# Attention into two expert layers: later routing constants, earlier weight splits, products with v behind six chunks, a turned chunk order

## The chip, the cores and the metric

The kernel runs on one core of a Trainium2 chip. The metric is the device time of one execution in microseconds; a kernel's time is the median of its runs. The five engines have in-order queues: TensorE (PE, with its weight loads PEld), VectorE (DVE), ScalarE (ACT), GpSimd (POOL), and SyncE (SP), which here only issues DMA.

## The reference

Three stages follow one another; the change touches the first and its hand-over to the second. The first is attention on 4 batches of 8 heads with 576 rows of 64 columns:

```python
def _attn_ref(q, k, v, tau):
    scale = 1.0 / np.sqrt(q.shape[-1])
    scores = scale * np.matmul(q, k.transpose(0, 1, 3, 2))
    thresh = np.max(scores, axis=-1, keepdims=True) - tau
    scores = np.where(scores >= thresh, scores, -1000000000.0)
    scores = scores - np.max(scores, axis=-1, keepdims=True)
    attn = np.exp(scores)
    attn = attn / (np.sum(attn, axis=-1, keepdims=True) + 1e-09)
    return np.matmul(attn, v).astype(np.float32)
```

The second sends each of the 2304 rows to the best of 8 experts (`np.maximum(xe @ w1[e], 0.0) @ w2[e]`, times the gate's probability), the third runs 4 further experts on every row and adds them up, weighted by `domain_probs`.

## The kernel before

Attention takes the heads two by two: 16 pairs, four to a batch. A pair's 576 rows of scores for two heads are cut into nine row chunks of 128: four for each head, and one (`None` in `full`, line 758) that holds the last 64 rows of both heads. `attention` (line 500) records all engines by hand in one loop over t = 0 to 148 (line 1100); one turn is called a step here, and t mod 9 its place in the pair. In step t, in this order:

- ACT takes the exponential of chunk t-1 (`expp`, line 794), PE multiplies q by k for chunk t+1 (`mm_s`, lines 776 and 777), DVE copies chunk t out of PSUM with its row maximum (`maxx`, line 785), and POOL makes the threshold `nm` from it (line 788).
- `late_setup` gives one piece (line 1125): small constants for routing, on POOL, then DVE.
- The next pair's q and k are split into high and low parts on POOL (`prep`, lines 569 and 572), and PE transposes those of the pair after this one in eight groups, `k0` to `l1` (line 698), two of them at place 1 and one at each place to 7. ACT copies each out (lines 646 to 696).
- DVE masks and sums chunk t-2 (`mask`, line 805).
- PE transposes the masked chunk t-4 (`transp`, lines 824 to 842), and ACT copies it into `PT` (lines 828 to 843).
- `xq` gives a step of a finished batch's routing (gate products, transposes, scatter into `xs`).
- At places 0 and 5 PE runs one half of an earlier pair's products of `PT` with v (`pv_items`, lines 859 and 865): 18 matmuls on 288 of the pair's 576 columns. DVE copies the result in the next step (line 876). `push_pv` (line 1088) queues both halves at place 4, after all nine chunks; the second half of a batch's fourth pair starts `after_batch`, that is routing.

All PE transposes and products of this loop go through one pool of four PSUM buffers in turn (`ps()`, line 516); the scores have two buffers of their own.

At the end of the loop the first weights of the first expert layer are split into high and low parts on POOL (`dosplit` and `split`, lines 360 and 362, at steps 140 and 143); the PE then works through the last chunks, the last pair's products, the last routing (`first_group`, line 1068) and the first products with these weights.

Of the kernel before, what the change touches and what calls it, by code (L numbers as in the profile page):

```python
# [11 lines left out]
F32 = mybir.dt.float32  # L12
F32R = mybir.dt.float32r
# [19 lines left out]
def kernel(  # L33
# [14 lines left out]
    nc = tc.nc  # L48
# [43 lines left out]
    def late_setup():  # L92
        nc.gpsimd.affine_select(
            out=tri, in_=ones, pattern=[[1, 128]], compare_op=ALU.is_gt, fill=0.0, base=0, channel_multiplier=-1
        )
        nc.gpsimd.iota(i8, pattern=[[1, 8]], base=0, channel_multiplier=0, allow_small_or_imprecise_dtypes=True)
        yield
        nc.vector.tensor_scalar(w8, i8, -1.0, 8.0, op0=ALU.mult, op1=ALU.add)
# [108 lines left out]
    def rank_consts():  # L207
        nc.gpsimd.iota(i16, pattern=[[1, 16]], base=0, channel_multiplier=0, allow_small_or_imprecise_dtypes=True)
        for r in range(8):
            nc.gpsimd.memset(cap[:, r : r + 1], float(CAP[r]))  # L210
        yield
        nc.vector.scalar_tensor_tensor(ck, reg0, -8.0, w8, op0=ALU.mult, op1=ALU.add)
        nc.vector.tensor_scalar(th, bc(i8, 1, 8), float(XW), None, op0=ALU.mult)
        nc.vector.tensor_tensor(th, th, bc(cap, 2, 8), op=ALU.add)
        nc.vector.tensor_tensor(low, bc(i8, 2, 8), bc(i8, 1, 8), op=ALU.is_gt)
# [133 lines left out]
    def place(i):  # L349
        return i < 4 or i // 2 % 2 == 1  # L350

    def raw_tile(i):
        return pools["wa" if place(i) else "wb"].tile([128, 1024], F32, tag="raw", name="raw", bufs=2)

    def split(raw, eH, eL, i):
# [144 lines left out]
    def attention(actx):  # L500
# [11 lines left out]
        NWARM = (36, 3, 3, 3)  # L512
        ET0 = 140
        g = nc.gpsimd
# [119 lines left out]
        def qk_groups(p):  # L634
# [62 lines left out]

            return [k0, k1, k2, q0, q1, q2, l0, l1]

# [58 lines left out]
        full = [(1, 0), (0, 0), (1, 1), (0, 1), (1, 2), (0, 2), (1, 3), (0, 3)]  # L758

        def order(p):  # L760
            return [None] + full if p == NPR - 1 else full + [None]

# [268 lines left out]
        setup = late_setup()  # L1031
        filling = fill(xe, 5)
        qk, pv, xq, dq, fq, po = deque(), deque(), deque(), deque(), [], []
        last = NPR - 1
# [52 lines left out]

        def push_pv(p, halves, deadline):
            b = p // 4
            for n, hf in enumerate(halves):  # L1090
                mm, ev = pv_items(p, hf)
                for f in mm:
                    pv.append((f, None, deadline))
                fin = None
                if p % 4 == 3 and n == len(halves) - 1:
                    fin = (lambda: after_batch(b)) if p != last else first_group
                pv.append((ev, fin, deadline))

        t = 0
        while t < NTT + LT + LP:  # L1100
# [5 lines left out]
            if t < NTT:  # L1106
# [16 lines left out]
                fpop()  # L1123
                if 11 <= t < 36:
                    next(setup, None)
# [15 lines left out]
            if u >= 0:  # L1141
                pp, ss = divmod(u, 9)
                if pp != last and ss == 8:
                    push_pv(pp, (0, 1), 9 * (pp + 2) + LT - 1)
                if pp == last and ss == 4:
                    push_pv(pp, (0,), t + 2)
            for _ in range(-(-len(qk) // (8 - s)) if 0 < s < 8 else 0):
                qk.popleft()()
            if 0 <= t - LT < NTT:
                transp(t - LT)  # L1150
            if t == ET0:
                dosplit(0, "g", "g")
                fetch(2)
            if t in (ET0 + 1, ET0 + 2):
                x_tr(*early["xr"][t - ET0 - 1], early["x"], ps)
            if t == ET0 + 3:
                dosplit(1, "g", "g")
                fetch(3)
            for _ in range(min(len(xq), 1 if t < NTT + LM else 3)):
                if xq[0] in frees or not fq and not busy and (xq[0] is not early_start or t >= 9 * last):  # L1160
                    xq.popleft()()
            if pv and (t % 9 in (0, 5) or t > 9 * last):
                d = pv[0][2]
# [477 lines left out]
```

## Time and profile before

| | |
|---|---|
| median of three runs | 1321.33 us (1319.15 to 1322.68) |
| the profiled execution | 1320.02 us, span 1318.1 us |
| busy share of the span | PE 98%, PEld 88%, DVE 66%, POOL 64%, ACT 49% |
| mean granted clock of TensorE | 0.995 of full speed |
| chain that ended last | PE 53%, waits for nothing shown 2%, POOL 1% |

The loop of attention fills the span from about 10 to 321 us, the first expert layer follows to about 550 us, the second takes the rest. PE is busy in nine tenths or more of nearly every slice of the span, so that what PE loses anywhere is lost at the end. A busy PE is not a PE at its peak: ends of matmuls are modelled, and a short wait can hide behind them. A wait is read from the row in which an engine starts: the square bracket at its end holds the idle time before it and what ended that.

### The profile page before, as it was taken

The page shows a single profiled execution, that of the slowest core. Times are in us where ns is not written, and L with a number is a line of the kernel's source. Part 1 is how long each engine was busy: PE and PEld are TensorE (multiplying, and loading weights), DVE is VectorE, ACT ScalarE, POOL GpSimd, SP SyncE. Part 2 cuts the span into 40 slices and gives each one's busy share as a digit, 9 for nine tenths or more (in the row PEclk, how much of TensorE's full clock was granted, in tenths as well). Part 3 has the DMA queues.
Part 4 walks back from the last instruction along what each step waited for, and adds up shares of the span by engine and source line. Part 5 has one row for each costly group of instructions (what it writes and reads, how often), then busy time and mean ns, then how long its engine had stood idle before and what let it go on. Part 6 is the DMA issues. An engine that isn't in the chain of part 4 may idle for free.

```text
span 1318.1 us, 22000 instructions
## 1 busy us (share of the span) xinstructions
PE 1294.5 (98%) x7928; PEld 1155.9 (88%) x7928; DVE 863.5 (66%) x1773; ACT 640.6 (49%) x1239; POOL 848.2 (64%) x937
## 2 busy tenths in 40 slices
PE   8999999999999999999999999999999999999997
PEld 7788788786999999989999999999999999999996
DVE  8888889887834357765655557556565675555654
ACT  7788888875554455643333334433333343333321
POOL 8776877754485442677667755777676667766642
PEclk8999999999999999999999999999999999999999
DMA  4542112113674556631221111222211122221101
GB/s 147 181 145 77 60 57 77 33 34 109 194 216 154 165 175 186 201 102 67 88 70 64 65 64 65 80 86 103 68 65 64 64 73 80 90 93 66 64 16 48
DMA packets 131534, 127.15 MB, mean 96 GB/s; under 512 B 17920, under 2 KB 110080, under 8 KB 131424
## 3 DMA queue, kind: packets, MB, share of 16 engines
q1 hardware_dynamic: 127968, 116.22, 27.8%
q0 software_dynamic: 3456, 9.51, 1.9%
q8 instruction: 63, 1.03, 0.3%
q14 instruction: 47, 0.39, 0.1%
HBM read 107.28 MB, written 18.42 MB: 95 GB/s over the span
## 4 chain that ended last, share of the span: by engine, by line
PE 53%; issue 2%; POOL 1%; ACT 0%; POOLq 0%; DVE 0%; ACTq 0%; DVEq 0%
PE w L370 9%; PE w L368 9%; PE w L369 9%; PE w L1487 8%; PE w L1489 8%; PE w L1488 8%; POOL out_dram L194 0%; POOL v2hl L1251 0%; POOL hl L1251 0%; ACT v2hl L1290 0%; ACT hl L1266 0%; POOLq L1636 0%; ACT yc L1301 0%; POOL pad L193 0%; DVE w L1495 0%
## 5 line engine op out<-in xcount | busy, mean ns | idle before, releaser
L1251 POOL TENSOR_TENSOR v2hl<-raw,v2hl 128x1024 fp32r<-128x1024 f32 x48 | 116.0, 2417 | 183.3 <-ACT v2hl L1290 183.3
L1562 DVE SCALAR_TENSOR_TENSOR y<-w,big,y 128x512 f32<-128x512 f32 x252 | 184.7, 747 | 75.1 <-PE w L370 73.9
L1487 PE MATMUL w<-yc,hl 128*128 128x384 f32 x672 | 225.6, 336 | 3.2 <-DVE y L425 1.8
L1489 PE MATMUL w<-yc,hl 128*128 128x384 f32 x672 | 225.5, 336 | 0.0
L1488 PE MATMUL w<-yc,hl 128*128 128x384 f32 x672 | 225.3, 335 | 0.0
L370 PE MATMUL w<-v2hl,g 128*128 128x512 f32 x576 | 224.8, 390 | 0.0
L368 PE MATMUL w<-v2hl,g 128*128 128x512 f32 x576 | 224.7, 390 | 0.0
L369 PE MATMUL w<-v2hl,g 128*128 128x512 f32 x576 | 224.4, 390 | 0.0
L1500 ACT ACTIVATE g<-w 128x384 fp32r<-128x384 f32 x192 | 94.4, 492 | 231.1 <-DVE w L1495 158.5
L1290 ACT CAST v2hl<-raw 128x1024 fp32r<-128x1024 f32 x48 | 50.4, 1050 | 220.2 <-PE w L370 204.5
L362 POOL TENSOR_TENSOR hl<-raw,hl 128x1024 fp32r<-128x1024 f32 x40 | 96.6, 2417 | 93.2 <-ACT hl L358 82.4
L1501 DVE SCALAR_TENSOR_TENSOR g<-w,g 128x384 fp32r<-128x384 f32 x192 | 106.5, 555 | 58.8 <-ACT g L1500 54.1
L805 DVE SCALAR_TENSOR_TENSOR P<-sb,nm,E 128x576 f32<-128x576 f32 x144 | 131.6, 914 | 10.4 <-POOL nm L788 3.7
L1487 PEld LDWEIGHTS w<-yc,hl 128*128 128x128 f32 x672 | 126.2, 188 | 5.7 <-issue 1.9
L370 PEld LDWEIGHTS w<-v2hl,g 128*128 128x128 f32 x576 | 108.1, 188 | 23.1
L1488 PEld LDWEIGHTS w<-yc,hl 128*128 128x128 f32 x672 | 126.2, 188 | 1.7
L369 PEld LDWEIGHTS w<-v2hl,g 128*128 128x128 f32 x576 | 108.1, 188 | 21.4
L368 PEld LDWEIGHTS w<-v2hl,g 128*128 128x128 f32 x576 | 108.2, 188 | 21.1
L1489 PEld LDWEIGHTS w<-yc,hl 128*128 128x128 f32 x672 | 126.2, 188 | 0.0
L788 POOL TENSOR_SCALAR nm<-nm,sc 128x1 f32<-128x1 f32 x144 | 82.3, 571 | 67.5 <-DVE sb L785 43.1
L1251 POOL TENSOR_TENSOR hl<-sx,hl 128x1024 fp32r<-128x1024 f32 x47 | 113.3, 2411 | 14.1 <-ACT hl L1266 14.1
L1251 POOL TENSOR_TENSOR hl<-raw,hl 128x512 fp32r<-128x512 f32 x94 | 95.5, 1038 | 38.8 <-ACT hl L1266 38.5
(308 smaller groups left out, 3023.1 us busy)
## 6 DMA issues: line engine op xcount, KB each, us to landing
raw<-in_moe_w_dram SPq DMA_DIRECT2D x168, 512.0 KB
xs<-zrow SPq DMA_DIRECT2D x32, 256.0 KB
kt<-in_k_dram SPq DMA_DIRECT2D x16, 256.0 KB
qt<-in_q_dram SPq DMA_DIRECT2D x16, 256.0 KB
vt<-in_v_dram SPq DMA_DIRECT2D x16, 256.0 KB
xrow<-xs SPq DMA_DIRECT2D x15, 256.0 KB
kt<-in_k_dram SPq DMA_DIRECT2D x16, 32.0 KB
qt<-in_q_dram SPq DMA_DIRECT2D x16, 32.0 KB
```

The lines of the kernel that those rows point to most:

```text
L362: e.tensor_tensor(hl[:, 1, :], raw, hl[:, 0, :].bitcast(F32), op=ALU.subtract)
L368: nc.tensor.matmul(o, lhsT=aH, rhs=bH, start=first, stop=False)
L369: nc.tensor.matmul(o, lhsT=aH, rhs=bL, start=False, stop=False)
L370: nc.tensor.matmul(o, lhsT=aL, rhs=bH, start=False, stop=last)
L805: nc.vector.scalar_tensor_tensor(P, sb, nm[:, 1:2], e, op0=ALU.is_le, op1=ALU.mult, accum_out=a)
L1251: e.tensor_tensor(o, a, b_, op=ALU.subtract)
L1487: nc.tensor.matmul(o, lhsT=aH, rhs=bH, start=first, stop=False, skip_group_check=True)
L1488: nc.tensor.matmul(o, lhsT=aH, rhs=bL, start=False, stop=False, skip_group_check=True)
L1489: nc.tensor.matmul(o, lhsT=aL, rhs=bH, start=False, stop=last, skip_group_check=True)
L1500: nc.scalar.activation(o[0], src, AF.Relu)
L1501: return lambda: nc.vector.scalar_tensor_tensor(o[1], src, 0.0, o[0].bitcast(F32), op0=ALU.max, op1=ALU.subtract)
L1562: nc.vector.scalar_tensor_tensor(d, w3(o), s_, d, op0=ALU.mult, op1=ALU.add)
```

## The change

Five edits, all in or around the loop of attention:

1. `late_setup` starts at step 20, not 11, and waits a step more between the POOL and the DVE instructions of its two groups of constants.
2. The first two weight splits start at step 137 (`ET0`), not 140, and `split_early` gives two of their eight pieces in each step. The low part of each is computed in two halves of 512 columns.
3. A pair's first half of the products with v is queued once six of its row chunks are transposed, and runs at place 1; the second half runs at place 5. Routing of a finished batch so starts four steps sooner.
4. In odd batches, whose columns lie in another order, the chunks are taken in the order 1, 2, 3, 0 and the second half of the columns comes first.
5. For the last pair, `l1` and `l0` change places.

```diff
--- before.py
+++ after.py
@@ -95,6 +95,7 @@
         )
         nc.gpsimd.iota(i8, pattern=[[1, 8]], base=0, channel_multiplier=0, allow_small_or_imprecise_dtypes=True)
         yield
+        yield
         nc.vector.tensor_scalar(w8, i8, -1.0, 8.0, op0=ALU.mult, op1=ALU.add)
         nc.vector.tensor_scalar(reg0, i8, float(NTOK), None, op0=ALU.mult)
         nc.vector.tensor_copy(base, reg0)
@@ -209,6 +210,7 @@
         for r in range(8):
             nc.gpsimd.memset(cap[:, r : r + 1], float(CAP[r]))
         yield
+        yield
         nc.vector.scalar_tensor_tensor(ck, reg0, -8.0, w8, op0=ALU.mult, op1=ALU.add)
         nc.vector.tensor_scalar(th, bc(i8, 1, 8), float(XW), None, op0=ALU.mult)
         nc.vector.tensor_tensor(th, th, bc(cap, 2, 8), op=ALU.add)
@@ -352,6 +354,17 @@
     def raw_tile(i):
         return pools["wa" if place(i) else "wb"].tile([128, 1024], F32, tag="raw", name="raw", bufs=2)
 
+    def split_early(i):
+        raw = raws.pop(i)
+        hl = hls[i] = pools["wa"].tile([128, 2, 1024], F32R, tag="hl", name="hl", bufs=2)
+        nc.gpsimd.tensor_scalar(hl[:, 0, :], raw, 1.0, 1.0, op0=ALU.mult, op1=ALU.mult)
+        yield
+        for x in (slice(0, 512), slice(512, 1024)):
+            nc.gpsimd.tensor_tensor(hl[:, 1, x], raw[:, x], hl[:, 0, x].bitcast(F32), op=ALU.subtract)
+            yield
+        fetch(i + 2)
+        yield
+
     def split(raw, eH, eL, i):
         hl = pools["wa" if place(i) else "wb"].tile([128, 2, 1024], F32R, tag="hl", name="hl", bufs=2)
         if eH == "a":
@@ -510,7 +523,7 @@
         DX = 1
 
         NWARM = (36, 3, 3, 3)
-        ET0 = 140
+        ET0 = 137
         g = nc.gpsimd
 
         def ps():
@@ -695,7 +708,7 @@
                     r = slice(h * 64, h * 64 + 64)
                     cp_(qLm[p % 2][r, h, 4, r], m[r, r])
 
-            return [k0, k1, k2, q0, q1, q2, l0, l1]
+            return [k0, k1, k2, q0, q1, q2] + ([l1, l0] if p == NPR - 1 else [l0, l1])
 
         def qk_first():
 
@@ -757,8 +770,12 @@
 
         full = [(1, 0), (0, 0), (1, 1), (0, 1), (1, 2), (0, 2), (1, 3), (0, 3)]
 
+        turned = [(h, c) for c in (1, 2, 3, 0) for h in (1, 0)]
+
         def order(p):
-            return [None] + full if p == NPR - 1 else full + [None]
+            if p == NPR - 1:
+                return [None] + full
+            return (turned if p // 4 % 2 else full) + [None]
 
         def mm_s(t):
             p, s = divmod(t, 9)
@@ -1030,6 +1047,7 @@
         NTT = 9 * NPR
         setup = late_setup()
         filling = fill(xe, 5)
+        weights = (None for i in range(2) for _ in split_early(i))
         qk, pv, xq, dq, fq, po = deque(), deque(), deque(), deque(), [], []
         last = NPR - 1
 
@@ -1085,14 +1103,14 @@
                 ]
             )
 
-        def push_pv(p, halves, deadline):
+        def push_pv(p, halves, deadline, whole=True):
             b = p // 4
             for n, hf in enumerate(halves):
                 mm, ev = pv_items(p, hf)
                 for f in mm:
                     pv.append((f, None, deadline))
                 fin = None
-                if p % 4 == 3 and n == len(halves) - 1:
+                if p % 4 == 3 and n == len(halves) - 1 and whole:
                     fin = (lambda: after_batch(b)) if p != last else first_group
                 pv.append((ev, fin, deadline))
 
@@ -1121,7 +1139,7 @@
                 maxx(t)
                 settle()
                 fpop()
-                if 11 <= t < 36:
+                if 20 <= t < 45:
                     next(setup, None)
                 if 6 <= t < 54 and s not in (0, 6):
                     next(filling, None)
@@ -1140,26 +1158,25 @@
             u = t - LT - LP
             if u >= 0:
                 pp, ss = divmod(u, 9)
+                if pp != last and ss == 5:
+                    push_pv(pp, (pp // 4 % 2,), t + 3, False)
                 if pp != last and ss == 8:
-                    push_pv(pp, (0, 1), 9 * (pp + 2) + LT - 1)
+                    push_pv(pp, (1 - pp // 4 % 2,), t + 3)
                 if pp == last and ss == 4:
                     push_pv(pp, (0,), t + 2)
             for _ in range(-(-len(qk) // (8 - s)) if 0 < s < 8 else 0):
                 qk.popleft()()
             if 0 <= t - LT < NTT:
                 transp(t - LT)
-            if t == ET0:
-                dosplit(0, "g", "g")
-                fetch(2)
-            if t in (ET0 + 1, ET0 + 2):
-                x_tr(*early["xr"][t - ET0 - 1], early["x"], ps)
-            if t == ET0 + 3:
-                dosplit(1, "g", "g")
-                fetch(3)
+            if t >= ET0:
+                next(weights, None)
+                next(weights, None)
+            if t in (ET0 + 4, ET0 + 5):
+                x_tr(*early["xr"][t - ET0 - 4], early["x"], ps)
             for _ in range(min(len(xq), 1 if t < NTT + LM else 3)):
                 if xq[0] in frees or not fq and not busy and (xq[0] is not early_start or t >= 9 * last):
                     xq.popleft()()
-            if pv and (t % 9 in (0, 5) or t > 9 * last):
+            if pv and (t % 9 in (1, 5) or t > 9 * last):
                 d = pv[0][2]
                 n = 5 if t <= 9 * last else -(-sum(x[2] == d and x[0].__name__ != "ev" for x in pv) // max(1, d + DX - t))
                 while pv and (n or pv[0][0].__name__ == "ev"):
```

Three places show how this moves the instructions. First, PE's queue around step 27, place 0. P23 and P24 are masked chunks, PT1 and PT2 the transposed chunks of pairs 1 and 2, s29 the scores of chunk 29, kHL4 the split k of pair 4, and each t_ one of the four PSUM buffers. Before:

```order
L824 MATMUL t_1193<-ident_62,P23_1131 128x128 x4
L831 MATMUL t_1199<-ident_62,P22_1097 128x128
L832 MATMUL t_1199<-ident_62,P23_1131 64x128
L859 MATMUL t_1203<-PT1_698,vl0_116 128x288
L865 MATMUL t_1203<-PT1_698,vt1_457 64x288 x8
L776 MATMUL s29_1215<-kT3_861,qHT1_119 128x288
...
L626 MATMUL t_1230<-identr_63,kHL4_872 128x128 x3
L626 MATMUL t_1235<-identr_63,kHL4_872 128x128 x3
L824 MATMUL t_1241<-ident_62,P24_1161 128x128 x4
```

and in the change:

```order
L841 MATMUL t_1183<-ident_62,P23_1110 128x128 x4
L848 MATMUL t_1189<-ident_62,P22_1076 128x128
L849 MATMUL t_1189<-ident_62,P23_1110 64x128
L793 MATMUL s29_1195<-kT3_839,qHT1_119 128x288
...
L639 MATMUL t_1216<-identr_63,kHL4_850 128x128 x3
L639 MATMUL t_1221<-identr_63,kHL4_850 128x128 x3
L841 MATMUL t_1227<-ident_62,P24_1144 128x128 x4
L876 MATMUL t_1233<-PT2_1004,vl0_116 128x288
L882 MATMUL t_1233<-PT2_1004,vt2_753 64x288 x8
```

The half of pair 1 behind chunk 23 is gone, and a half of pair 2 stands one step later, behind two groups of k (`k0`, `k1`) and chunk 24.

Second, DVE's queue where the first routing constants are made (w8, reg0 and base from i8, which POOL fills). Before, at step 12:

```order
L785 TENSOR_SCALAR sb12_649,nm12_650<-s12_612 128x576
L98 TENSOR_SCALAR w8_67<-i8_66 128x8
L99 TENSOR_SCALAR reg0_68<-i8_66 128x8
L100 COPY base_69<-reg0_68 128x8
L805 SCALAR_TENSOR_TENSOR P10_659,rs0_130<-sb10_584,nm10_585,E10_610 128x576
L785 TENSOR_SCALAR sb13_684,nm13_685<-s13_644 128x576
L102 MEMSET M_74 128x144
L805 SCALAR_TENSOR_TENSOR P11_691,rs0_130<-sb11_617,nm11_618,E11_642 128x576
```

and in the change, at step 22:

```order
L802 TENSOR_SCALAR sb22_988,nm22_989<-s22_951 128x576
L99 TENSOR_SCALAR w8_67<-i8_66 128x8
L100 TENSOR_SCALAR reg0_68<-i8_66 128x8
L101 COPY base_69<-reg0_68 128x8
L822 SCALAR_TENSOR_TENSOR P20_997,rs0_130<-sb20_923,nm20_924,E20_949 128x576
L802 TENSOR_SCALAR sb23_1018,nm23_1019<-s23_983 128x576
L103 MEMSET M_74 128x144
L822 SCALAR_TENSOR_TENSOR P21_1026,rs0_130<-sb21_956,nm21_957,E21_981 128x576
```

The three instructions stand behind the copy of chunk 22's scores, not of chunk 12's; POOL fills i8 two steps before them, not one.

Third, PE's queue at the end of the loop. P143 is the last chunk, PT14 and PT15 are the last two pairs, LG the gate products of the last batch, outT0 to outT3 its attention output. Before:

```order
L824 MATMUL t_5243<-ident_62,P143_5221 128x128 x4
L832 MATMUL t_5249<-ident_62,P143_5221 64x128
L865 MATMUL t_5207<-PT14_4788,vt14_4508 64x256 x2
L859 MATMUL t_5256<-PT15_5079,vl1_117 128x320
L865 MATMUL t_5256<-PT15_5079,vt15_4843 64x320 x8
L859 MATMUL t_5267<-PT15_5079,vl1_117 128x256
L886 MATMUL t_5269<-outT0_124,wg_129 32x320
...
L886 MATMUL t_5269<-outT3_127,wg_129 32x320
L865 MATMUL t_5267<-PT15_5079,vt15_4843 64x256 x2
L925 MATMUL t_5281<-ident_62,LG_128 128x128
L865 MATMUL t_5267<-PT15_5079,vt15_4843 64x256 x2
```

and in the change:

```order
L841 MATMUL t_5259<-ident_62,P143_5234 128x128 x4
L849 MATMUL t_5265<-ident_62,P143_5234 64x128
L903 MATMUL t_5269<-outT0_124,wg_129 32x320
...
L903 MATMUL t_5269<-outT3_127,wg_129 32x320
L942 MATMUL t_5279<-ident_62,LG_128 128x128
L942 MATMUL t_5284<-ident_62,LG_128 128x128 x2
L963 MATMUL t_5299<-ident_62,outT0_124 128x128
...
L963 MATMUL t_5299<-ident_62,outT3_127 128x128
L876 MATMUL t_5306<-PT15_5095,vl1_117 128x256
```

The products of pairs 14 and 15 that stood between and behind these now stand ahead of the last chunk; the gate products follow it directly, and the transposes of LG follow them with nothing between.

## Rows read from the trace of the kernel before

**Rows 1.** Windows: busy us of PE, PEld, DVE, ACT, POOL, granted clock, DMA share, GB/s.

```profile
25.00:50.00 25.00, 21.48 (x156) 16.73 (x156) 21.41 (x56) 19.01 (x44) 20.46 (x54) 0.93 0.58 172
...
100.00:150.00 50.00, 49.91 (x417) 41.05 (x416) 43.61 (x122) 40.55 (x94) 36.20 (x63) 1.00 0.26 78
...
300.00:350.00 50.00, 48.01 (x370) 36.07 (x367) 38.64 (x107) 27.46 (x55) 21.90 (x25) 1.00 0.38 118
...
700.00:1318.00 618.00, 610.76 (x3069) 552.83 (x3067) 372.08 (x605) 210.63 (x358) 397.44 (x343) 1.00 0.20 70
```

**Rows 2.** Whom PE waited for, 0 to 360 us: total us, times, longest.

```profile
PE s L776 <- DVE sb L785: 5.0, 8, 2.5
...
PE s L777 <- ACT qLm L696: 0.3, 1, 0.3
```

**Rows 3.** Timeline of PE, steps 11 to 15: start us, us, instruction.

```profile
30.79 0.40 PE L776 MATMUL s<-kT,qHT 128*128 128x288 f32 x1 [0.48 <-DVE sb L785]
...
32.71 0.40 PE L776 MATMUL s<-kT,qHT 128*128 128x288 f32 x1 [0.23 <-DVE sb L785]
...
36.71 0.40 PE L776 MATMUL s<-kT,qHT 128*128 128x288 f32 x1 [2.53 <-DVE sb L785]
...
38.27 1.17 PE L859 MATMUL t<-PT,vl 128*128 128x288 f32 x2
...
42.54 0.40 PE L776 MATMUL s<-kT,qHT 128*128 128x288 f32 x1
```

**Rows 4.** Window within step 14, columns as in rows 1.

```profile
38.00:40.00 2.00, 2.00 (x10) 1.00 (x10) 1.90 (x9) 2.00 (x5) 1.51 (x12) 0.55 0.50 133
```

**Rows 5.** Timeline of DVE, steps 12 to 16.

```profile
33.65 0.55 DVE L98 TENSOR_SCALAR w<-i 128x8 f32<-128x8 f32 x1 [1.00 <-POOL i L96]
...
34.68 1.29 DVE L805 SCALAR_TENSOR_TENSOR P<-sb,nm,E 128x576 f32<-128x576 f32 x1
...
39.45 0.30 DVE L212 SCALAR_TENSOR_TENSOR ck<-reg,w 128x8 f32<-128x8 f32 x1
...
40.73 0.81 DVE L805 SCALAR_TENSOR_TENSOR P<-sb,nm,E 128x576 f32<-128x576 f32 x1
```

**Rows 6.** Timeline of PE, end of step 23 and steps 27 to 29.

```profile
57.65 0.27 PE L832 MATMUL t<-ident,P 128*64 128x128 f32 x1
57.97 0.75 PE L859 MATMUL t<-PT,vl 128*128 128x288 f32 x2
...
65.97 0.27 PE L832 MATMUL t<-ident,P 128*64 128x128 f32 x1
66.08 0.65 PE L859 MATMUL t<-PT,vl 128*128 128x288 f32 x2
...
68.75 0.40 PE L776 MATMUL s<-kT,qHT 128*128 128x288 f32 x1
...
69.86 0.63 PE L824 MATMUL t<-ident,P 128*128 128x128 f32 x4
70.24 0.38 PE L776 MATMUL s<-kT,qHT 128*128 128x288 f32 x1
```

**Rows 7.** Timeline of ACT, steps 22 to 27.

```profile
57.23 0.69 ACT L828 COPY PT<-t 128x512 f32<-128x512 f32 x1
...
61.88 1.18 ACT L632 CAST qLm<-t 64x512 fp32r<-64x512 f32 x2 [1.59 <-PE t L626]
...
67.13 0.59 ACT L828 COPY PT<-t 128x512 f32<-128x512 f32 x1
```

**Rows 8.** Timeline of POOL, second weight split.

```profile
317.35 2.73 POOL L362 TENSOR_TENSOR hl<-raw,hl 128x1024 fp32r<-128x1024 f32 x1
```

**Rows 9.** Timeline of DVE, the mask of the last chunk.

```profile
317.81 2.89 DVE L805 SCALAR_TENSOR_TENSOR P<-sb,nm,E 128x576 f32<-128x576 f32 x1
```

**Rows 10.** Timeline of PE, the last chunk's transposes.

```profile
320.86 0.63 PE L824 MATMUL t<-ident,P 128*128 128x128 f32 x4 [1.61 <-DVE P L805]
```

**Rows 11.** Timeline of ACT, the copy of the last batch's gate products.

```profile
326.72 0.42 ACT L890 COPY LG<-t 128x320 f32<-128x320 f32 x1 [4.45 <-PE t L886]
```

## The prediction

> **What bounds the kernel now.** I read the windows first [rows 1]. From 700 us to the end PE is busy for 610.8 of 618 us at full clock, and between 100 and 150 us for 49.9 of 50. There a change that moves instructions can win nothing. Two stretches of the attention loop have room: 25 to 50 us, where PE is busy for 21.5 of 25 us at a mean clock of 0.93 while DVE and POOL are busy for over 20 us each, and 300 to 350 us, with 2 us idle. Next, whom PE waited for [rows 2]: in the first 360 us it waits most for the copy of the scores, 5.0 us in eight waits, and one wait of 2.5 us is half of that. So PE sets the time, and the question for each edit is how much of PE's waiting it removes or makes.
>
> **Part 1: constants later, and a half of the products at step 10.** Steps 11 to 14 hold three of the eight waits, 0.48, 0.23 and 2.53 us [rows 3]. The idle time counts from a modelled end: four transposes are on record for 0.63 us, but the next group starts 0.38 us after them when nothing is in the way, as from 69.86 to 70.24 us [rows 6], so each wait is some 0.2 us longer, 3.9 us in all. The long one is made by the constants: DVE, in order, stands 1.00 us before w8 because POOL has not yet filled i8, and spends another 1.03 us on the three small instructions before the next mask, from 33.65 to 34.68 us [rows 5]; the copy of chunk 13 queues behind these, and PE behind that. Behind the wait comes a second loss: the first products with v last from 38.27 to 42.54 us, 4.27 us [rows 3], at a granted clock of 0.55 [rows 4], near the lower of its two levels (1.2 of 2.4 GHz), after PE had stood still; the same 18 matmuls at full clock last 2.67 us, from 66.08 to 68.75 [rows 6]. That is 1.6 us more, 5.5 us together.
>
> In the change the constants are gone from these steps, and a half of the products, 2.67 us of PE, moves from step 18 to step 10. I followed the queues through steps 10 to 15 with these durations: while PE works on the half, DVE and POOL catch up, and none of the three waits comes back. So I take **-5.5 us**. The lower end is 3.6 us: the constants' 2.03 us on DVE and the slow clock's 1.6 us go, the rest stays.
>
> The constants now stand at steps 22 and 26: 1.03 us and, from 39.45 to 40.73, 1.28 us of DVE [rows 5]. Their cover is the half of the products at steps 23 and 28, in which DVE has nothing else to do; without it the 2.3 us are PE's wait. POOL's fill comes two steps ahead, so DVE should not wait for it. I take **+0.3**, between 0 and 2.3.
>
> **Part 2: splits sooner.** The last mask lasts 2.89 us [rows 9] where another, at 40.73, lasts 0.81 [rows 5]: it starts 0.46 us after POOL's low part of the second split, which lasts 2.73 us [rows 8], and ends 0.6 us behind it. PE waits 1.61 us for that mask [rows 10], about 1.8 with the modelled end. With the splits at steps 137 to 140 POOL is done before the last masks: **-1.8**, between 0 and that. The two fetches behind the splits are issued earlier; no row shows PE waiting for them, so I cost them at nothing.
>
> **Part 3: what covers the end.** In the change nothing stands on PE between the gate products and the transposes of LG, which need ACT's copy, 0.42 us [rows 11]; with the way to ACT and back I estimate 0.7 us. The route's small DVE steps come after that and lose some cover too, 0.3. I take **+1.0**, between 0 and 1.8.
>
> **Part 4: the last pair's l1 before l0.** PE waits once for the copy of `l1`, 0.3 us [rows 2], about 0.4 with the modelled end. The new order gives that copy a step more: **-0.4**.
>
> **Part 5: the steady state, which speaks against the change.** ACT is behind PE between a half at place 5 and the next half. It starts the copies of `l0` at 61.88 us [rows 7] and has no gap up to chunk 23's copy, which ends at 67.72. Before, PE ran a half meanwhile, from 66.08 us [rows 6]. In the change it goes on to s29, k0, k1 and chunk 24, which takes 1.11 us when nothing waits, as from 68.75 to 69.86 [rows 6]; it would transpose chunk 24 at 67.19. But the four PSUM buffers go round: k0, k1 and the small transposes of chunk 23 take three, and chunk 24 needs the one that chunk 23's copy frees at 67.72. PE starts 0.05 us after such a copy, as at 57.97 behind a copy that ended at 57.92 [rows 6, 7]. So it waits about 0.6 us, once in each pair. From step 19 to step 127 there are 13 such places; at five of them (46, 82, 91, 118, 127) a batch's routing puts transposes of its own on PE, ACT is not that far behind, and I take none. 8 x 0.6 = **+4.8**, between 0 and 13 x 0.6 = 7.8.
>
> In exchange the half at place 5 has four steps of ACT's lag before it, not five: there PE starts 0.32 us behind the last transposes, against 0.11 at place 0 (57.65 to 57.97, 65.97 to 66.08 [rows 6]). The trace has six halves with those 0.2 us: **-1.2**. Routing starts four steps sooner; its instructions are the same, they only meet other ones: 0, within 1.5 either way. The turned chunk order changes no count and no duration: 0.
>
> **Sum.** -5.5 + 0.3 - 1.8 + 1.0 - 0.4 + 4.8 - 1.2 = -2.8 us. Against the profiled execution, 1320.02 us, that is 1317.2; its time lies 1.3 us below the median of the three runs, so against the median I forecast **1318.5 us**.
>
> **The rivals.**
>
> *A. No wait for PSUM in part 5.* If ACT's work at place 0 comes sooner than I read it, the 4.8 us go: -7.6, **1313.7 us**. For it: in the trace before no step shows PE waiting at chunk 24's place. Against: there a half always stood in front.
>
> *B. The same wait, twice as long (the slower side).* The half at place 1 also needs chunk 23's small copy in `PT`, one step old, and ACT's exponentials wait in turn for masks. At 1.2 us in each of the 13 places part 5 costs 15.6, not 4.8: +8.0, **1329.3 us**. It decides for slower from a mean wait of 0.9 us on, where the sum is +4. The Trainium skill (Perfetto Trace Analysis, Optimization Strategy) says that the same gap repeating on the engine that should be saturated can mean too few buffers in SBUF or PSUM. By that rule part 5 would show as one gap in every pair; the trace before has it only as the 0.2 us at place 5.
>
> *C. POOL's pieces hold up the masks.* Low parts of two times 2.73 us, the high parts and the thresholds now fill POOL in steps 137 to 140, when masks are made every step. If a mask stands still for each piece as the last one did [rows 8, 9], the masks fall behind by more than the two steps that they have in hand: nothing is won, and PE waits as long again, +3.6, **1322.1 us**. The Trainium skill (SBUF — State Buffer, 🔬 SBUF: two separate sides) says that a DVE instruction with two SBUF inputs and a GpSimd instruction that reads SBUF lock each other out, for the whole instruction. The trace agrees: the mask ended 0.6 us behind POOL's 2.73. Against C: a half part holds a lock for half as long, and PE has products with v in each of these steps.
>
> *D. The first part doesn't do what it says.* If DVE and POOL set the pace of steps 10 to 14 even without the constants, 3.6 us are won, not 5.5: -0.9, **1320.4 us**.
>
> **Chances.** My forecast 0.40, A 0.27, D 0.14, C 0.12, B 0.07. About 0.3%, 4 us, is what a measurement of this kernel tells from no change. A lies beyond that, and a third of my own case does with its bounds: faster 0.39. C, D and the rest of my case lie within: 0.55. Slower 0.06, nearly all of it B. The range goes from 1312.5 (A with a little more won at the end) to 1323.5 (C with the constants' cover lost in part); B is left out.
>
> **What would show it.** Right: no wait above 0.5 us on PE between 28 and 45 us, and a clock of 1.0 there; at each place 1 that is not in routing, transposes of PE that start 0.05 us behind ACT's copy, some 0.6 us late; no wait for the last mask; a gap of about 0.7 us before the transposes of LG. Wrong: no gap at place 1 (A), a gap above 0.9 (B), masks of over 1.5 us with PE waiting in steps 137 to 143 (C), or waits for the scores that remain in steps 11 to 14 (D).

## The result, and the profile after

The changed kernel takes 1328.53 us (1327.73 to 1329.34, six runs), the kernel before 1320.77 us beside it (six runs): a ratio of 1.006, 95% interval 1.0049 to 1.0071. It is slower by 7.8 us; I had forecast 1318.5 us and a range up to 1323.5, so the result lies 10.0 us above the forecast.

The profiled execution took 1329.2 us. Its page begins:

```profile
span 1327.4 us, 22005 instructions
...
PE 1296.2 (98%) x7928; PEld 1157.2 (87%) x7928; DVE 863.3 (65%) x1773; ACT 643.9 (49%) x1239; POOL 845.8 (64%) x939
```

The windows that answer to [rows 1], and the one within step 14 [rows 4], with the same columns:

```profile
25.00:50.00 25.00, 24.19 (x191) 19.12 (x190) 20.69 (x55) 21.33 (x49) 22.34 (x41) 1.00 0.78 256
100.00:150.00 50.00, 43.40 (x352) 36.70 (x349) 41.17 (x113) 36.13 (x83) 32.57 (x61) 0.96 0.25 77
300.00:350.00 50.00, 47.56 (x358) 34.38 (x356) 38.14 (x119) 29.20 (x63) 20.59 (x32) 1.00 0.35 112
38.00:40.00 2.00, 2.00 (x18) 1.07 (x15) 0.64 (x3) 1.23 (x3) 2.00 (x3) 1.00 0.42 123
```

The first stretch is filled, as I had said: PE is busy for 24.2 of 25 us at full clock, and in step 14 the clock is 1.00 where it was 0.55. But from 100 to 150 us, where PE had no room, it now has 6.6 us of idle time. Whom PE waited for from 0 to 360 us [rows 2]:

```profile
PE s L793 <- DVE sb L802: 9.0, 10, 5.6
PE t L841 <- ACT PT L845: 2.3, 5, 0.5
PE t L942 <- issue: 1.3, 1, 1.3
...
PE t L942 <- ACT LG L907: 0.6, 1, 0.6
PE t L152 <- DVE oh L149: 0.4, 1, 0.4
```

One wait of 5.6 us is new. To see when the time was lost I took PE's start of the scores of the same chunk in both traces (us; a negative difference is a lead of the changed kernel). Where it has done one half of a pair's products more (2.67 us [rows 6]), that is taken off as well:

| point | before | after | difference | with the half counted | since the point above |
|---|---|---|---|---|---|
| chunk 17 | 43.85 | 40.99 | -2.86 | -5.5 | -5.5 |
| chunk 40 | 89.89 | 88.47 | -1.42 | -4.1 | +1.4 |
| chunk 64 | 141.40 | 140.73 | -0.67 | -3.3 | +0.8 |
| chunk 66 | 146.83 | 154.41 | +7.58 | +4.9 | **+8.2** |
| chunk 100 | 219.01 | 226.53 | +7.52 | +4.9 | 0 |
| chunk 106 | 233.17 | 243.53 | +10.36 | +7.7 | **+2.8** |
| expert layer, first use of `he` | 344.63 | 353.54 | +8.9 | +8.9 | +1.2 |
| span | 1318.1 | 1327.4 | +9.3 | +9.3 | +0.4 |

So 8.2 us go between chunks 64 and 66. PE there (start, us, instruction):

```profile
141.35 0.60 PE L841 MATMUL t<-ident,P 128*128 128x128 f32 x4
...
147.73 0.61 PE L793 MATMUL s<-kT,qHT 128*128 128x288 f32 x1 [5.56 <-DVE sb L802]
...
150.45 1.17 PE L876 MATMUL t<-PT,vl 128*128 128x288 f32 x2
151.54 2.93 PE L882 MATMUL t<-PT,vt 128*64 128x288 f32 x16
154.41 0.40 PE L793 MATMUL s<-kT,qHT 128*128 128x288 f32 x1
```

PE waits 5.56 us for a copy of scores, and afterwards the half at place 1 takes 3.96 us, from 150.45 to 154.41, not 2.67: after the standstill the clock is at its lower level, 1.2 GHz, as the windows of these microseconds show (columns as above):

```profile
148.00:150.00 2.00, 2.00 (x12) 1.98 (x13) 2.00 (x7) 1.34 (x4) 1.66 (x4) 0.50 0.49 134
150.00:152.00 2.00, 2.00 (x8) 1.08 (x8) 1.29 (x4) 1.62 (x4) 1.91 (x4) 0.50 0.14 34
152.00:154.00 2.00, 2.00 (x14) 1.09 (x12) 0.00 (x0) 0.00 (x0) 0.00 (x0) 0.71 0.00 0
```

DVE, which owes the copy:

```profile
143.48 1.69 DVE L822 SCALAR_TENSOR_TENSOR P<-sb,nm,E 128x576 f32<-128x576 f32 x1 [3.17 <-POOL nm L805]
...
145.10 1.60 DVE L188 TENSOR_TENSOR sg<-sg,sp__2419 128x4 f32<-128x4 f32 x1
...
146.92 0.75 DVE L802 TENSOR_SCALAR_CACHE_REDUCE sb<-s 128x576 f32<-128x576 f32 x1
```

It stands 3.17 us at a mask whose threshold POOL has not made; the copy queues behind, and behind two long instructions: the mask takes 1.69 us, not 0.81 [rows 5], and the small one of line 188 takes 1.60 (last section). And POOL:

```profile
135.77 0.24 POOL L582 TENSOR_SCALAR kHL<-kt 64x64 fp32r<-64x64 f32 x1 [1.31 <-DMA xs<-X,desti]
...
136.47 1.06 POOL L195 DMA_INDIRECT xs<-X,desti  x1 [0.30 <-issue]
137.62 0.29 POOL L805 TENSOR_SCALAR nm<-nm,sc 128x1 f32<-128x1 f32 x1
140.65 0.32 POOL L585 TENSOR_TENSOR kHL<-kt,kHL 64x64 fp32r<-64x64 f32 x1 [2.75 <-DMA xs<-X,desti]
...
142.01 1.08 POOL L195 DMA_INDIRECT xs<-X,desti  x1 [0.15 <-issue]
143.14 0.30 POOL L805 TENSOR_SCALAR nm<-nm,sc 128x1 f32<-128x1 f32 x1
...
145.28 1.39 POOL L585 TENSOR_TENSOR qL<-qt,qH 128x256 fp32r<-128x256 f32 x2
```

This is the head of the chain. POOL issues routing's scatters (line 195) and splits the next pair's q and k (`prep`, lines 582 and 585). Two pieces of 64x64 on the upper partitions, each issued behind a scatter, stand still until it has landed: 1.31 us, and 2.75 us behind the scatter of 136.47. Behind them, and behind one more scatter of 1.08 us, waits the threshold of 143.14. Their shape doesn't make them wait: among the semaphores on which an instruction waits, the trace has those of the scatters for these two pieces, but also for the 128x256 instruction of 145.28, which didn't stand still, and not for the upper 64x64 piece of 147.29. In the kernel before, batch 0's scatters lay four steps later against the same pieces, and its PE was busy for 19.91 of the 20 us from 130 to 150.

Theory 1 is this chain. Rival 2 is the wait for PSUM at place 1 (part 5 and rival B of the prediction); rival 3, that routing's work on DVE and ACT costs where it lies now; theory 4, added after the first four runs, that POOL's stalls cost what no half on PE covers.

### The profile page after: what moved, and what is told of

Same layout as the page of the kernel before. It is cut to its first block, busy times and chain, and to the rows that moved or that the text cites. A ratio compares the mean times of both kernels' runs of the same rounds, so it can differ in the third digit from the quotient of the medians.

```text
span 1327.4 us, 22005 instructions
## 1 busy us (share of the span) xinstructions
PE 1296.2 (98%) x7928; PEld 1157.2 (87%) x7928; DVE 863.3 (65%) x1773; ACT 643.9 (49%) x1239; POOL 845.8 (64%) x939
## 4 chain that ended last, share of the span: by engine, by line
PE 53%; issue 2%; POOL 1%; ACT 0%; POOLq 0%; DVE 0%; ACTq 0%; DVEq 0%
PE w L383 9%; PE w L381 9%; PE w L382 9%; PE w L1504 8%; PE w L1506 8%; PE w L1505 8%; POOL out_dram L195 0%; POOL v2hl L1268 0%; POOL hl L1268 0%; ACT v2hl L1307 0%; ACT hl L1283 0%; POOLq L1653 0%; ACT yc L1318 0%; POOL pad L194 0%; DVE w L1512 0%
## 5 line engine op out<-in xcount | busy, mean ns | idle before, releaser
L375 POOL TENSOR_TENSOR hl<-raw,hl 128x1024 fp32r<-128x1024 f32 x38 | 91.1, 2400 | 94.9 <-ACT hl L371 84.3
L805 POOL TENSOR_SCALAR nm<-nm,sc 128x1 f32<-128x1 f32 x144 | 79.1, 549 | 74.6 <-DVE sb L802 48.3
L811 ACT ACTIVATE E<-sb,nm 128x576 f32<-128x576 f32 x144 | 115.8, 804 | 10.5 <-DVE P L822 9.9
```

The lines of the kernel that those rows point to most:

```text
L811: nc.scalar.activation(e, sb, AF.Exp, bias=nm[:, 0:1], scale=-1.0)
```

## The experiments

Each was timed against the kernel before in the same runs, whose medians were 1320.0 to 1320.9 us. A difference between two changed kernels that were run in different sets is uncertain by about that much.

**Routing as late as before.** In `after_batch`, the other edits kept:

```diff
         def after_batch(b):
+            xq.extend([lambda: None] * 4)
             if b == B - 2:
```

> The changed kernel with four empty steps ahead of the routing of the first three batches, so that their routing starts where it did before. Theory 1: the time is lost because routing starts four steps sooner, so that POOL comes to a 64x64 split right behind a scatter and stands until the scatter has landed (1.31 and 2.75 us at 135 and 140 us), the thresholds come late and PE waits 5.56 us at 142 us and then runs slowly. Then the 8.2 us lost between chunks 64 and 66 and most of the 2.9 us lost at chunks 103 and 104 come back: 1318 to 1320 us. Rival 2: the loss is the wait for PSUM buffers at place 1, in every pair. Routing's place changes nothing of it: 1327 to 1330 us.

Measured 1323.88 us, ratio 1.0033 (1.0022 to 1.0043). The wait at 142 us is gone and 4.7 us come back, half of what theory 1 expected; the time lies between the two ranges. The lead over the kernel before, counted as in the table, falls slowly, from 5.5 us at chunk 17 to 1.65 at 237 us; then some 4 us go at once, in batch 1. POOL there:

```profile
234.92 0.24 POOL L582 TENSOR_SCALAR kHL<-kt 64x64 fp32r<-64x64 f32 x1 [1.59 <-DMA xs<-X,desti]
...
239.06 0.32 POOL L585 TENSOR_TENSOR kHL<-kt,kHL 64x64 fp32r<-64x64 f32 x1 [2.01 <-DMA xs<-X,desti]
```

and PE:

```profile
242.96 0.55 PE L793 MATMUL s<-kT,qHT 128*128 128x288 f32 x1 [2.57 <-DVE sb L802]
...
245.61 1.08 PE L876 MATMUL t<-PT,vl 128*128 128x288 f32 x2
```

The kernel before has the same two stalls at the same pieces, and its PE waits only 0.29 us. POOL before:

```profile
233.75 0.26 POOL L569 TENSOR_SCALAR kHL<-kt 64x64 fp32r<-64x64 f32 x1 [1.58 <-DMA xs<-X,desti]
...
237.63 0.32 POOL L572 TENSOR_TENSOR kHL<-kt,kHL 64x64 fp32r<-64x64 f32 x1 [1.75 <-DMA xs<-X,desti]
```

and PE before, at place 0 behind the stall:

```profile
237.76 0.40 PE L776 MATMUL s<-kT,qHT 128*128 128x288 f32 x1 [0.29 <-DVE sb L785]
...
239.05 0.65 PE L859 MATMUL t<-PT,vl 128*128 128x288 f32 x2
239.63 2.16 PE L865 MATMUL t<-PT,vt 128*64 128x288 f32 x16
```

A half starts there 1.4 us after POOL goes on; with place 1 it started 6.6 us after. From this came theory 4.

**The upper pieces on DVE.** Nine instructions of pairs 8, 12 and 13; `e2` stands for `e1` in the two lines of k, and the low part of q's last chunk likewise:

```diff
...
+                e2 = nc.vector if h and p in (8, 12, 13) else e1
...
```

> The changed kernel, routing as soon as there, but the 64x64 split pieces on partitions 64 to 127 of pairs 8, 12 and 13 (nine instructions of about 0.3 us) on DVE instead of POOL. Theory 1: POOL then has no wait for a scatter in steps 59 to 64 and 102 to 105, the 5.56 us wait of PE at 142 us is gone with the slow clock behind it, and DVE's nine pieces cost under 1 us: 1318 to 1321 us. Rival 3: routing itself, met by other work of DVE and ACT four steps sooner, is what costs, and the scatter's wait on POOL only shows it: 1325 us or more, with PE still waiting for score copies between 135 and 150 us. Rival 2 (PSUM at place 1): 1327 to 1330.

Measured 1322.33 us, 1.0016 (1.0006 to 1.0025): 6.2 us less than the changed kernel, 1.3 above theory 1's range and below that of rival 3. POOL waits for no scatter in batches 0 and 1 any more, and PE's wait of 5.56 us shrinks to two of 1.57 and 0.74. Ahead of these stand DVE's added pieces and two long DVE instructions beside POOL, a mask of 1.63 us and one of 1.54 (last section). Between chunks 100 and 106, in batch 1, this kernel loses 1.4 us, counted as in the table, where the changed kernel lost 2.8.

**The same pieces earlier, on POOL.** Only pair 8's order:

```diff
             st["prep", p] = (qH, qL, kHL)
+            if p == 8:
+                ops = ops[2:4] + ops[6:8] + ops[0:2] + ops[4:6] + ops[8:]
             return ops
```

> The changed kernel with one pair's split in another order: for pair 8 the four 64x64 pieces of k come first, two steps before the first scatter of batch 0, and not behind the second and third. No instruction is added, removed or put on another engine. Theory 1 (POOL stands at these pieces until the scatter has landed, 1.31 and 2.75 us, and that makes the loss between chunks 64 and 66): the 5.56 us wait of PE at 142 us and the slow clock behind it are gone, 8 us less than the changed kernel, 1319.5 to 1321.5; batch 1's loss of 2.9 us stays. Rival 3 (routing's own work on DVE and ACT costs): 1326 or more.

Measured 1322.03 us, 1.0013 (1.0003 to 1.0023): 6.5 us less, with the same instructions on the same engines; 8 were expected, and the time lies 0.5 above theory 1's range. POOL waits for no scatter in batch 0. PE at the place of the long wait:

```profile
141.80 0.40 PE L795 MATMUL s<-kT,qHT 128*128 128x288 f32 x1 [0.69 <-DVE sb L804]
...
144.33 0.40 PE L795 MATMUL s<-kT,qHT 128*128 128x288 f32 x1 [1.08 <-DVE sb L804]
```

The clock is 1.00 from 130 to 150 us. Theory 1 holds for batch 0; 1.8 us of waits for DVE's copies are left, and the loss in batch 1 stays, 2.9 us between chunks 100 and 106.

**The products alone** (the diff's parts from `turned` on and in `push_pv`, that is edits 3 and 4, in the kernel before) and **the constants alone** (its first two parts and `20 <= t < 45`, edit 1):

> The kernel before with the products moved and the turned order alone (edits 3 and 4); constants and weight splits stay where they were. Theory 1: the early routing comes with this edit alone, so the whole loss of some 10 us is in it; the half at step 10 still takes up a part of the waits of steps 11 to 14 (2 to 4 us): 1327 to 1332 us. If the loss came from the constants at steps 22 and 26 or from the splits at 137, this kernel would show 1317 to 1322.

Measured 1330.05 us, 1.0079 (1.0056 to 1.0102): the whole loss is in this edit, with a wait of 5.45 us at 148 us. But the steps 11 to 14 are cured here too, with the constants still in their old place. PE there:

```profile
36.45 0.40 PE L780 MATMUL s<-kT,qHT 128*128 128x288 f32 x1 [0.30 <-DVE sb L789]
```

The wait of 2.53 us is gone, the clock from 38 to 40 us is 1.00, and chunk 17 starts 4.6 us ahead, counted as in the table.

> The kernel before with the constants later alone (edit 1). If the constants make the wait of 2.53 us at step 14 and the slow clock behind it by themselves: 2.0 and 1.6 us go, some 1317 us. If the half at step 10 is what fills the steps, and DVE and POOL set the pace there even without the constants: 1319.5 to 1321.

Measured 1315.55 us, 0.9965 (0.9952 to 0.9977). PE's waits of 0.48 and 0.23 us in steps 11 and 12 stay; the long one and the slow clock go. Chunk 17 starts 3.7 us sooner than before, though this execution began its loop 0.46 us later: 4.2 us won, and kept to the end of the loop.

**Constants, splits and l1** (those parts, and `split_early` with what calls it, `ET0` and the order of l1 and l0):

> The kernel before with edits 1, 2 and 5: constants later, weight splits in pieces from step 137 on, l1 before l0 for the last pair. The products stay in their places. Part 2 right: PE's wait of 1.6 us for the last mask, still there with the constants alone, is gone, and 1.8 + 0.4 us come off the 1315.6 us of that run: 1313 to 1314.5. Rival C (POOL's pieces hold up the masks at the loop's end): 1315.5 to 1318, with masks of over 1.5 us and PE waiting in steps 137 to 143.

Measured 1313.40 us, 0.9949 (0.9930 to 0.9968), **the fastest of all**. PE's wait for the last mask is gone, and the first products of the expert layer start at 324.16 us, with the constants alone at 326.60. Of these 2.4 us this execution was 0.7 ahead since its start (a wait at the same place comes at 147.28 here and at 148.00 there); 1.7 are won at the end. PE's wait for the copy of `l1`, 0.3 us with the constants alone, is gone too.

**Routing five steps later.** In the changed kernel:

```diff
         def after_batch(b):
+            xq.extend([lambda: None] * (5 if b < 2 else 4))
             if b == B - 2:
```

> The changed kernel with five empty steps ahead of the routing of the first two batches (four for the third). With four, 4.5 us were still lost at chunks 107 to 109, where PE waited 2.57 us at 243 us for scores behind POOL's wait for a scatter, and the half of the products came only after that. Theory 4: what counts is whether a half follows on PE right where POOL stands; one step later than with four, routing lies to the halves at places 1 and 5 as it lay before to those at 0 and 5, the half then covers the wait: 1319 to 1321 us. Theory 1 alone (it is only the place of POOL's 64x64 pieces against the scatters, and there are still three such pieces right behind scatters of batch 1): 1323 to 1326.

Measured 1327.42 us, 1.0050 (1.0032 to 1.0068): neither. POOL's stalls in batch 1 are of the same length (1.83 and 1.51 us), but PE waits 4.93 us at 245 us, and its next half starts only at 248.17. That it would lie as before was wrong, since routing moved against the splits too. POOL and PE there:

```profile
238.35 0.32 POOL L585 TENSOR_TENSOR kHL<-kt,kHL 64x64 fp32r<-64x64 f32 x1 [1.51 <-DMA xs<-X,desti]
...
239.72 1.08 POOL L195 DMA_INDIRECT xs<-X,desti  x1 [0.16 <-issue]
```

```profile
245.46 0.61 PE L793 MATMUL s<-kT,qHT 128*128 128x288 f32 x1 [4.93 <-DVE sb L802]
```

Why it lost more than with four steps can be read from the two traces, though no run tested it. A scatter now stands between the piece and the next threshold, which comes 2.50 us after the piece went on, not 1.16; and DVE's small instruction of line 188 comes ahead of the copy and takes 1.61 us beside POOL, where with four steps it came earlier and took 0.16. The long wait of the changed kernel has both as well.

**Parts of 256 and 320 columns at places 0 and 5.** On edits 1, 2 and 5, with routing held back four steps:

```diff
-        turned = [(h, c) for c in (1, 2, 3, 0) for h in (1, 0)]
+        turned = [(h, c) for c in (3, 2, 1, 0) for h in (1, 0)]
...
-            e = 320 if b == B - 1 else 288
+            e = 320 if b % 2 else 256
...
+            xq.extend([lambda: None] * 4)
...
-                if pp != last and ss == 5:
+                if pp < last - 1 and ss == 3:
...
-                if pp != last and ss == 8:
+                if pp < last - 1 and ss == 8:
...
+                if pp == last - 1 and ss == 8:
+                    push_pv(pp, (0, 1), 9 * (pp + 2) + LT - 1)
...
-            if pv and (t % 9 in (1, 5) or t > 9 * last):
+            if pv and (t % 9 in (0, 5) or t > 9 * last):
```

> Edits 1, 2 and 5 as in the first kernel of this call, and the products in another way: the first part of a pair's products takes 256 columns, which need only four chunks, and runs at place 0; the other takes 320, at place 5; routing is held back four steps, so that it starts as in the kernel before; the pair before the last keeps its old place, so that the end is covered as before. Odd batches take the chunks 3, 2, 1, 0. If place 1 with its full PSUM buffers and the missing cover at place 0 made the loss of some 8 us that is left beside the early routing: no creeping loss from pair to pair, and the part at step 9 wins up to 1.8 us in steps 11 to 14: 1311 to 1314 us. If earlier products cost for any other reason (ACT, DVE or PT copies): 1316 us or more, with the lead over the kernel before falling from pair to pair.

Measured 1314.11 us, 0.9950 (0.9934 to 0.9967). The lead is between 5.4 and 5.7 us from chunk 17 to the scatters of batch 0 and 4.9 to 5.2 up to chunk 124: it does not fall from pair to pair. POOL stands at batch 1's pieces for 1.73 and 1.51 us as before, and PE loses nothing there, having a part at 236.84. But about 1 us goes at the end of the loop, and the sum is no better than without moving the products: just above the range, where up to 1.8 us had been hoped for.

**The same, with the last batch's pairs in their old places:**

```diff
-                if pp < last - 1 and ss == 3:
+                if pp < last - 3 and ss == 3:
...
-                if pp < last - 1 and ss == 8:
+                if pp < last - 3 and ss == 8:
...
-                if pp == last - 1 and ss == 8:
+                if last - 3 <= pp < last and ss == 8:
```

> The kernel with parts of 256 and 320 columns at places 0 and 5 and routing held back, but the pairs of the last batch queue their products as in the kernel before. In the run with all pairs moved, the lead over the kernel before was 5.2 us up to chunk 120 and fell by some 1.2 us between chunks 124 and 142, where PE waited for scores and had no products left to do. If that missing part is the cause, it comes back: 1312 to 1313.3 us, below the 1313.4 of constants and splits alone. If not: 1314 as with all pairs moved.

Measured 1314.24 us, 0.9952 (0.9938 to 0.9965): a miss. The lead fell by 0.9 us already where the old places begin, near 257 us.

**Routing sooner alone.** The kernel with parts at 0 and 5, without the four empty steps:

```diff
         def after_batch(b):
-            xq.extend([lambda: None] * 4)
             if b == B - 2:
```

> The kernel with parts of 256 and 320 columns at places 0 and 5 (1314.1 us), without the four empty steps ahead of routing: routing alone starts four steps sooner, and nothing else changes. POOL then meets the scatters of batch 0 with its 64x64 pieces as in the changed kernel. Theory 1 (the scatter's wait on POOL costs by itself, 8 and 3 us as there): 1322 to 1326 us. Theory 4 (it costs what no part of the products on PE covers; here a part stands at place 0, one step nearer to the stall): the wait of 5.56 us shrinks to about 3, 1317 to 1320 us. If early routing costs nothing without the waits at place 1: 1314.

Measured 1322.93 us, 1.0008 (0.9996 to 1.0020): **8.8 us more for early routing alone**, nothing else changed (three of the ten runs took 1320.5 to 1320.8 us). PE where batch 0's scatters are:

```profile
140.67 0.60 PE L876 MATMUL t<-PT,vl 128*128 128x256 f32 x2
141.20 1.95 PE L882 MATMUL t<-PT,vt 128*64 128x256 f32 x16
146.25 0.40 PE L793 MATMUL s<-kT,qHT 128*128 128x288 f32 x1 [3.11 <-DVE sb L802]
```

The part at place 0 covers 2.4 us of the stall and the wait is 3.11, as theory 4 had said. The time is theory 1's: batch 1 adds waits of 1.49 and 0.71 us at 231 and 233 us, and the end one of 1.33.

**The same with pair 8's pieces first:**

> The same order of pair 8's pieces in the kernel with parts of 256 and 320 columns at places 0 and 5 and early routing (1322.9 us). There chunks 64 to 66 lost about 4.5 us to POOL's wait, PE waiting 3.11 us at 146 us. Theory 1: these come back and batch 1's share of some 3 to 4 us stays: 1318 to 1319.5. Rival 3: 1322 or more.

Measured 1318.83 us, 0.9988 (0.9977 to 0.9999): 4.1 us back. The wait of 3.11 is now 0.38, batch 1's waits stay, 1.59 and 0.72 us, and so does that of 1.33 at the end. So 4.7 of the 8.8 us are left.

**The end as before**, in the changed kernel:

```diff
-                if pp != last and ss == 5:
+                if pp < last - 1 and ss == 5:
...
-                if pp != last and ss == 8:
+                if pp < last - 1 and ss == 8:
...
+                if pp == last - 1 and ss == 8:
+                    push_pv(pp, (0, 1), 9 * (pp + 2) + LT - 1)
```

> The changed kernel with the products of the last pair but one queued as in the kernel before (both halves after nine chunks), so that they lie at the end of the loop. In the changed kernel PE stands 0.57, 0.41 and 1.28 us around the transposes of LG, which before were covered. If that cover is the cause: 2 to 2.5 us less than the changed kernel, 1325.5 to 1326.5. If the end's waits come from elsewhere (DVE's routing steps): 1328.

Measured 1327.42 us, 1.0050 (1.0033 to 1.0067), 1.1 us less. The three waits around LG are gone, so the cover was their cause; but PE waits 1.34 us for scores at 313.51, where it now has less to do, and half the gain goes there.

## Why the prediction was wrong

**The step that failed** is the sentence in part 5 "Routing starts four steps sooner; its instructions are the same, they only meet other ones: 0, within 1.5 either way". With the parts at places 0 and 5 it is worth +8.8 us by itself; in the changed kernel the 8.2 and 2.8 us of the table lie where the scatters are, but holding routing back gave only 4.7 us, since the half at place 1 then came too late for batch 1. I had counted instructions and not asked what POOL does behind a scatter. The trace of before showed it, in rows that I had not read: POOL's stalls of 1.58 and 1.75 us in batch 1, and one of 0.68 in batch 0. Those of batch 1 cost PE at most its wait of 0.29 us there, and a half stood on PE right behind them. In batch 0 all four scatters moved, two pieces came to stand right behind scatters, and the half came too late. Shown: the chain from the pieces to PE in batch 0, by three edits; one pair's order alone gave back 6.5 of the 10.0 us between forecast and result. For batch 1 less is shown: the run that took its pieces off POOL lost half as much there, but it added work to DVE. Why the program makes some POOL instructions wait for scatters wasn't tried. I had given a slower kernel a chance of 0.06, nearly all for rival B, which is not what happened.

**Part 1** (-5.5): chunk 17 starts 5.5 us ahead. The constants alone bring 4.2 of it, between my lower end of 3.6 and the whole, and leave two waits (0.48 and 0.23 us); the products alone bring 4.6 with the constants in their old place. So either edit removes the long wait and the slow clock, and what they win doesn't add up: my account, that the constants make the wait and the half then covers the rest, gave the sum and missed this. Rival D was closer on what the constants do, and wrong on the sum. The constants' new place costs more than +0.3, within its bounds: DVE makes `ck`, `th` and `low` from 61.54 us on, and PE waits 0.57 us at 64.28, after which the lead is 0.7 us smaller.

**Part 2** (-1.8) came out at -1.7 in the run with edits 1, 2 and 5. The low parts last 1.27 to 1.66 us, the masks at the loop's end 0.8 to 1.2, the last one 0.81, against 2.73 and 2.89 before [rows 8, 9]: not rival C. **Part 4** was not timed by itself; the wait for `l1` is not among those after.

**Part 3** (+1.0, at most 1.8) had only one of three gaps right. PE at the end:

```profile
333.45 0.55 PE L942 MATMUL t<-ident,LG 128*128 128x128 f32 x3 [0.57 <-ACT LG L907]
...
336.29 0.19 PE L152 MATMUL t<-oh,tri 128*128 128x24 bf16 x1 [0.41 <-DVE oh L149]
...
342.25 0.44 PE L942 MATMUL t<-ident,LG 128*128 128x128 f32 x2 [1.28 <-issue]
```

The first gap is the one I had priced, 0.57 us. The last, 1.28 us, stands before the transposes of the other half of LG, which were covered by the route's small products and four transposes before; I had followed only the first half. The three add up to 2.26 us, above my bound, but giving the cover back won only 1.1 us, about what I had put: that is luck, since a wait of 1.34 us came up in another place.

**Part 5, PSUM at place 1**, held in mechanism and about in size. In the trace after (PE, a chunk's transposes behind k0 and k1):

```profile
46.72 0.66 PE L841 MATMUL t<-ident,P 128*128 128x128 f32 x4 [0.53 <-ACT PT L845]
...
83.86 0.66 PE L841 MATMUL t<-ident,P 128*128 128x128 f32 x4 [0.52 <-ACT PT L845]
```

With routing as late as before, whom PE waited for from 0 to 360 us:

```profile
PE t L841 <- ACT PT L845: 3.9, 8, 0.5
```

Seven of the eight are of 0.5 us, one of 0.2. That eight is the count that I had given is partly luck: they stand at steps 19, 37, 46, 64, 73, 82, 100 and 118, so three are at places where I had taken none (46, 82, 118), and three of mine (28, 55, 109) have none. The lead there falls from 5.5 to 1.65 us. Of these 3.8 us, 0.7 are the constants', and the other 3.1 stand against my +4.8 and -1.2. With the parts at places 0 and 5 the lead does not fall. The Trainium skill (Perfetto Trace Analysis, Optimization Strategy) holds that a gap which repeats on the engine that should be busy can mean too few buffers; the trace agrees, with a gap of 0.5 us at seven of thirteen places, each ended by the copy that empties a buffer. No run changed the number of buffers.

**Rival B** gave 1329.3 us, 0.8 from the result, and is wrong all the same: it needed a mean wait of 0.9 us at place 1, and the waits are 0.5.

## What to carry to other kernels

When a step moves, look at every queue for waits that are hidden now, not only at those on the engine that sets the time: a stall on POOL that costs nothing may be covered by what happens to run beside it, and both can move. Work that issues transfers on a compute engine's queue needs its distance to whatever waits for them there; one pair's pieces in another order gave back 6.5 us. And time the edits apart, since they need not add up: the constants, the splits and the order of l1 and l0 take 7.5 us off the kernel before, which makes 1313.4 us, 0.5% faster; from the kernel with the products moved, 1330.05 us, they take 1.5.

## What the runs showed of the hardware

A scatter of 128 rows occupies POOL for 1.05 to 1.67 us in the loops of the traces before and after; the 64x64 piece that waited for the one of 136.47 us went on at 140.65, some 4 us after its start.

A DVE instruction on a tile of 128x4 lasted nearly ten times its usual time beside POOL. With the pieces on DVE:

```profile
139.82 1.54 DVE L185 TENSOR_SCALAR sg<-sg 128x4 f32<-128x4 f32 x1
...
141.49 0.14 DVE L185 TENSOR_SCALAR sp__2419<-sp__2419 128x4 f32<-128x4 f32 x1
```

and POOL in the same run:

```profile
139.93 1.41 POOL L585 TENSOR_TENSOR qL<-qt,qH 128x256 fp32r<-128x256 f32 x2
```

The first ends 0.02 us behind POOL's two instructions; the second, alike but without POOL beside it, takes 0.14. The Trainium skill (SBUF — State Buffer, 🔬 SBUF: two separate sides) says that a DVE instruction and one of GpSimd lock each other out of a shared port for a whole instruction, if the DVE one runs in a two-port mode, or has two SBUF inputs and the one of GpSimd reads SBUF. The trace of the changed kernel agrees for two inputs: the DVE instruction of line 188, 1.60 us from 145.10, ended 0.03 us behind POOL's two of 145.28, which lasted 1.39. The instruction shown above has one input; whether it ran in a two-port mode no trace shows.
